# Attention and mixer kernel on one core: hand order kept through the first block's steps, conversions of weights between softmax steps, weight transfers three entries ahead

## Chip, core and metric

The kernel runs on one core of a Trainium2 chip. The metric is device microseconds of one execution; a kernel is timed several times and the median is given. A profile is taken in an execution of its own.

## What is computed

```
# q, k, v: (8 batches, 8 heads, 576, 64), chunks of 64 along the sequence
scores = scale * matmul(q_c, k_c^T)                    # 64 x 64 per chunk
attn   = softmax(scores); x = matmul(attn, v_c)        # back to (8, 576, 512)
h      = relu(x^T @ w_tok1) @ w_tok2                   # 576 -> 256 -> 576, over the sequence
u      = x + h^T
out    = u + relu(u @ w_ch1) @ w_ch2                   # 512 -> 1536 -> 512, over the channels
```

The four weight matrices come in double precision. Everything else is in single precision.

## The kernel before

**The matmuls.** A product is made of three matmuls in fp32r, a reduced form of fp32: a number is split into a kept half and a low half, and kept×kept, kept×low and low×kept are added (`THREE`). The kept half is a ScalarE cast; the low half is the number less the kept one, on VectorE (on GpSimd for `xl`).

**Channel part.** The 4608 columns of the eight batches are cut into nine blocks of 512. A block has twelve steps f. In step f, `ch1` (L534) multiplies `u` by a slice of 128 columns of w_ch1 (twelve matmuls at L540), ScalarE writes the kept half of the relu, `gh` (L545), and VectorE the low half, `gl` (L546). `ch2` (L553) multiplies these by the matching slice of w_ch2 (twelve matmuls at L568) into four accumulators. On TensorE, `ch2` of step f - 1 stands behind `ch1` of step f. At a block's end VectorE and GpSimd add `u` and the sync queue writes the output (L577, L579, L584). `SEGMENTS` gives the order: steps 0 to 7 of block 0, all of block 1, steps 8 to 11 of block 0, then blocks 2 to 8.

**Attention and token part.** A tile is two chunks, 128 rows of the sequence, with eight heads. Two batches make nine tiles: four of the one, the fifth half and half, four of the other. The first five are worked ahead of everything (L619 to L646), with transposes on TensorE. The later ones are put into steps of the channel part, given by `SLOTS`; for block 0 these are steps 0, 2, 4 and 6. `attention(k)` (L657) finishes tile j and begins the next tile, i: `pt` of j (L344, ScalarE), scores of i and the product with V of j in one PSUM tile (`attn_both`, L285, L305), loads of a later tile, the row maximum `mx` (L266), the difference (L269), the exponential (L273, ScalarE), the transposition of the probabilities of i by way of DRAM (`attn_far`: VectorE transposes in blocks, L316, a store `far`, four loads into `pf`), the sums, and then for j the division (`attn_o`), `xh`, `xl` and a transposition of x by way of DRAM into `xt` (`attn_x`). Between two blocks, at a turn, `tok1` (L482, matmuls at L459) and `tok2` (L507, L522) make the `u` of the next block: `u` (L527, VectorE), `uh` (L531, ScalarE), `ul` (L532, VectorE). The first block has forms of its own (`tok1_first`, `tok2_first`). The fifth tile is stored half by half for its two batches (`ready`, `attn_stack`, with a cast at L417).

**The weights.** They are handed over as 64-bit words in 29 entries of `plan`: five for the token weights, then c1_0, c1_1, c2_0, c1_2, c2_1 and so on. `fetch` (L108) issues an entry's transfer on the sync queue, `AHEAD` entries ahead of its use, into one of `RAW_BUFS` buffers. The words become a single on the chip: ScalarE writes `wtop` and `low` (L131, L132, `words_scalar`, called by `prepare`), VectorE clamps (L135), puts the sign in (L148), shifts (L141) and adds (L155); then come the kept cast (L203, ScalarE) and the low half (L209, VectorE). `conversion` (L171) is a generator that issues the VectorE steps one at a time: clamp of entry i, sign of i - 1, shift of i, add of i - 1 (with its cast), low half of i - 2. `convert(n)` takes n of them; ten make two entries. `ch1` and `ch2` take as many as they still need for their slice.

**What sets the order.** The sync queue and TensorE follow the program's order all through. ScalarE and VectorE follow it only through the start (`by_hand`, closed at L648); from there on a scheduler orders them, with what the start issued kept in front. `FIRST_FILL`, `PREPARE` and `END_FILL` say how many conversions stand between the softmax steps of the start. `CONVERT` asks for ten per step in block 0 and four in block 1. The splits of the token weights (`split`, L682) are issued in step 5.

Of the kernel before, what the change touches and what calls it, by code (L numbers as in the profile page):

```python
# [16 lines left out]
P = 128  # L17
B, H, S, D = 8, 8, 576, 64
CH = 64
# [26 lines left out]
CONVERT = {(0, 0): 10, (1, 0): 4, (0, F0): 0}  # L46

AHEAD = 7
RAW_BUFS = 8
KEPT_GROUPS = (13, 21)  # L50
# [3 lines left out]
FIRST_FILL = (3, 4, 5, 5, 6)  # L54
PREPARE = (0, 2, 2, 2, 2)
END_FILL = (4, 3, 2)
# [3 lines left out]
def attention_mixer_kernel(ctx, tc, qk_in, v_in, w1_in, w2_in, wc1_in, wc2_in, out):  # L60
# [57 lines left out]
    def words_scalar(i):  # L118
# [194 lines left out]
    def far_out(src, tag="far"):  # L313
# [6 lines left out]
        far = dram.tile([P, DM], F32, tag=tag, name="far")  # L320
# [101 lines left out]
    def attn_x(b, i):  # L422

        for t, rows, j in mix_tiles(b):
# [3 lines left out]
            while first < end:  # L428
# [3 lines left out]
                far_in(tiles[t]["x"], xt(k)[:, at:at + n], part)  # L432
# [101 lines left out]
    def ch1(u, f):  # L534
# [3 lines left out]
        for k in range(NDT):  # L538
            for q, (wi, ui) in enumerate(THREE):
# [3 lines left out]
                )  # L543
        gh, gl = [pool.tile([P, N], F32R, tag=tag, name=tag) for tag in ("gh", "gl")]
# [69 lines left out]
    attn_load(first[4])  # L614
    warm(12)
# [27 lines left out]
    rs, us = {0: r}, {0: block_u()}  # L643
# [5 lines left out]
    after = ExitStack()  # L649
    for engine in engines:  # L650
        ins = [i for i in nc.cur_bb.bb.instructions if i.engine == engine][-1]
        after.enter_context(tc.issue_after(ins))

    attn_load(second[1])
    order = [t for b in range(1, B) for t in batch_tiles(b)]

    def attention(k):  # L657
# [8 lines left out]
        if i is not None:  # L666
            attn_p(i)
            attn_far(i)
            attn_z(i)
        if j is not None:  # L670
            attn_o(j)
            attn_end(j)
            for b in range(1, B):
                if j in [t for t, _, _ in mix_tiles(b)] and (b % 2 == 0 or j % NTILE != 4):
                    attn_x(b, j)
# [6 lines left out]
    def split():  # L682
        for i in range(token):
# [103 lines left out]
```

## Time and profile before

| | |
|---|---|
| Median of 3 runs | 834.29 us (833.8, 834.29, 835.13) |
| Profiled execution | 832.94 us, span 831.2 us |
| Mean granted TensorE clock | 0.967 |
| Busy share of the span: TensorE, VectorE, ScalarE, GpSimd | 94%, 45%, 26%, 10% |
| Chain that ended last | TensorE 82%, DMA 7%, VectorE 5%, ScalarE 2% |
| Start of `ch1` of step 0, block 0 | 56.42 us |
| End of `ch1` of step 7, block 0 | 134.41 us |

The span runs from the first instruction to the last; the execution's time is 1.7 us more. PE is TensorE, DVE VectorE, ACT ScalarE, POOL GpSimd, SPq the sync queue. A row of the timeline has the start, the duration, the engine, the line and operation, output and inputs, and in brackets the idle time ahead of it with what ended it. In a row of stretches the four busy engines follow the length.

### The profile page before, as it was taken

The page shows a single profiled execution, that of the slowest core. Times are in us where ns is not written, and L with a number is a line of the kernel's source. Part 1 is how long each engine was busy: PE and PEld are TensorE (multiplying, and loading weights), DVE is VectorE, ACT ScalarE, POOL GpSimd, SP SyncE. Part 2 cuts the span into 40 slices and gives each one's busy share as a digit, 9 for nine tenths or more (in the row PEclk, how much of TensorE's full clock was granted, in tenths as well). Part 3 has the DMA queues.
Part 4 walks back from the last instruction along what each step waited for, and adds up shares of the span by engine and source line. Part 5 has one row for each costly group of instructions (what it writes and reads, how often), then busy time and mean ns, then how long its engine had stood idle before and what let it go on. Part 6 is the DMA issues. An engine that isn't in the chain of part 4 may idle for free.

```text
span 831.2 us, 13454 instructions
## 1 busy us (share of the span) xinstructions
PE 780.8 (94%) x5552; PEld 633.7 (76%) x5552; DVE 374.7 (45%) x660; ACT 214.1 (26%) x361; POOL 86.1 (10%) x74
## 2 busy tenths in 40 slices
PE   6685679999999999999999999999999999999997
PEld 4354567888888888888888888888888888887886
DVE  4979786423534433454443435534442323115112
ACT  4655453212231222122322221222212211012100
POOL 0000100200210000211020011200030102004000
PEclk7696799999999999999999999999999999999999
DMA  9634654232463333145403340534133201001001
GB/s 358 237 123 140 204 200 143 83 97 83 140 186 106 103 107 123 53 151 159 140 28 123 127 137 16 171 129 160 32 118 118 77 1 51 0 1 50 1 1 51
DMA packets 67373, 89.90 MB, mean 108 GB/s; under 512 B 7984, under 2 KB 40240, under 8 KB 67312
## 3 DMA queue, kind: packets, MB, share of 16 engines
q1 hardware_dynamic: 67312, 89.05, 32.1%
q8 instruction: 43, 0.70, 0.4%
q14 instruction: 18, 0.15, 0.1%
HBM read 61.10 MB, written 27.00 MB: 106 GB/s over the span
## 4 chain that ended last, share of the span: by engine, by line
PE 82%; DMA 7%; DVE 5%; ACT 2%; SPq 1%; issue 1%; ACTq 0%; DVEq 0%
PE acc L568 35%; PE ps_c L540 33%; PE ps_t L522 6%; PE ps_t L459 5%; DMA raw<-in_wc 2%; PE ps_sv L293 2%; PE ps_sv L305 2%; DMA far<-blocks 2%; DMA qk<-in_qk 2%; DMA raw<-in_w 1%; SPq L327 1%; DVE u L527 1%; DVE wtop L148 1%; ACT wtop L131 1%; ACT low L132 1%
## 5 line engine op out<-in xcount | busy, mean ns | idle before, releaser
L568 PE MATMUL acc<-gh,kept 128*128 128x512 f32 x864 | 274.8, 400 | 0.0
L540 PE MATMUL ps_c<-uh,kept 128*128 128x512 f32 x864 | 267.8, 391 | 0.0
L546 DVE SCALAR_TENSOR_TENSOR gl<-ps_c,gh 128x512 fp32r<-128x512 f32 x108 | 74.5, 690 | 335.7 <-ACT gh L545 326.1
L540 PEld LDWEIGHTS ps_c<-uh,kept 128*128 128x128 f32 x864 | 162.9, 189 | 34.8
L568 PEld LDWEIGHTS acc<-gh,kept 128*128 128x128 f32 x864 | 161.9, 190 | 34.9
L568 PE MATMUL acc<-gl,kept 128*128 128x512 f32 x432 | 170.7, 395 | 0.0
L540 PE MATMUL ps_c<-ul,kept 128*128 128x512 f32 x432 | 168.8, 391 | 0.3 <-DVE ul L505 0.3
L545 ACT ACTIVATE gh<-ps_c 128x512 fp32r<-128x512 f32 x108 | 64.5, 597 | 316.6 <-PE ps_c L540 314.3
L568 PEld LDWEIGHTS acc<-gl,kept 128*128 128x128 f32 x432 | 82.4, 191 | 18.2
L540 PEld LDWEIGHTS ps_c<-ul,kept 128*128 128x128 f32 x432 | 81.4, 188 | 17.8 <-DVE ul L505 0.8
L402 POOL TENSOR_TENSOR xl<-x,xh 128x512 fp32r<-128x512 f32 x28 | 36.6, 1308 | 447.1 <-ACT xh L401 420.1
L579 POOL TENSOR_TENSOR o<-o,ul 128x512 f32<-128x512 f32 x32 | 43.5, 1388 | 236.9 <-DVE o L577 236.9
L522 PE MATMUL ps_t<-kept,rh 128*128 128x448 f32 (+7 forms) x224 | 49.6, 314 | 6.2 <-DVE u L527 6.2
L522 PEld LDWEIGHTS ps_t<-kept,rh 128*128 128x128 f32 x224 | 37.1, 189 | 9.3 <-DVE u L527 7.9
L305 PE MATMUL ps_sv<-v,pt 64*64 64x64 f32 x992 | 21.2, 225 | 22.8 <-ACT pt L344 22.8
L344 ACT COPY pt<-pf 128x512 f32<-128x512 f32 x31 | 19.2, 620 | 79.4 <-DMA pf<-far 79.4
L273 ACT ACTIVATE pr<-pr 128x512 f32<-128x512 f32 x36 | 22.7, 632 | 63.1 <-DVE pr L269 63.0
L531 ACT CAST uh<-u 128x512 fp32r<-128x512 f32 x32 | 19.9, 621 | 68.4 <-DVE u L527 68.4
L527 DVE TENSOR_TENSOR u<-ps_t,xt 128x512 f32<-128x512 f32 x32 | 22.1, 689 | 32.3 <-PE ps_t L522 32.0
L305 PEld LDWEIGHTS ps_sv<-v,pt 64*64 64x64 f32 x992 | 18.2, 140 | 23.8 <-ACT pt L344 23.4
L459 PE MATMUL ps_t<-xh,kept 128*128 128x512 f32 x112 | 34.9, 393 | 0.0
L522 PE MATMUL ps_t<-kept,rl 128*128 128x448 f32 (+7 forms) x112 | 34.7, 311 | 0.0
(74 smaller groups left out, 614.5 us busy)
## 6 DMA issues: line engine op xcount, KB each, us to landing
qk<-in_qk SPq DMA_DIRECT2D x36, 512.0 KB, 3.9
far<-blocks SPq DMA_DIRECT2D x63, 256.0 KB, 2.1
raw<-in_wc SPq DMA_DIRECT2D x24, 512.0 KB, 6.2
v<-in_v SPq DMA_DIRECT2D x36, 260.0 KB, 4.3
out<-o SPq DMA_DIRECT2D x32, 256.0 KB, 2.0
pf<-far SPq DMA_DIRECT2D x124, 64.0 KB, 1.9
xt<-far SPq DMA_DIRECT2D x96, 64.0 KB, 2.0
xt<-far SPq DMA_DIRECT2D x64, 32.0 KB, 1.8
```

What stands on the lines that cost most here:

```text
L273: nc.scalar.activation(out=pr, in_=pr, func=AF.Exp, scale=1.0 / float(D) ** 0.5)
L305: nc.tensor.matmul(ps[c * CH:(c + 1) * CH, a, (NHP + hp) * D:(NHP + hp + 1) * D], lhsT=t["pt"][a * CH:(a + 1) * CH, hp, c * CH:(c + 1) * C ...
L402: nc.gpsimd.tensor_tensor(out=xl, in0=t["x"], in1=xh.bitcast(F32), op=ALU.subtract)
L459: nc.tensor.matmul(ps, lhsT=lhsT, rhs=rhs, start=(n == 0 and q == 0), stop=(n == len(mt) - 1 and q == len(terms) - 1),)
L522: nc.tensor.matmul(ps[:, at:at + n], lhsT=lhsT[:, cols], rhs=rhs, start=(q == 0), stop=(q == len(terms) - 1),)
L527: nc.vector.tensor_tensor(out=u.rearrange("p (i c) -> p i c", c=BK), in0=ps.rearrange("p (i c) -> p i c", c=BK), in1=xt(k)[:, :, m], op=AL ...
L531: nc.scalar.copy(out=uh[:, m], in_=u)
L540: nc.tensor.matmul(ps, lhsT=weights["c1", f][:, wi, k * P:(k + 1) * P], rhs=u[ui][:, k], start=(k == 0 and q == 0), stop=(k == NDT - 1 and ...
L545: nc.scalar.activation(out=gh, in_=ps, func=AF.Relu)
L546: nc.vector.scalar_tensor_tensor(out=gl, in0=ps, scalar=0.0, in1=gh.bitcast(F32), op0=ALU.max, op1=ALU.subtract)
L568: nc.tensor.matmul(accs[e], lhsT=weights["c2", f][:, wi, e * P:(e + 1) * P], rhs=g[gi], start=(first and q == 0), stop=(end and q == 2),)
L579: nc.gpsimd.tensor_tensor(out=o, in0=o, in1=ul, op=ALU.add)
```

## The change

Numbers: `AHEAD` goes from 7 to 3, `RAW_BUFS` from 8 to 7; there are five buffers for `wtop` and four for `low`. `FIRST_FILL` falls from 23 conversions to 10, `END_FILL` from 4, 3 and 2 (the last four times) to 3, 3 and 2.

Order: ScalarE and VectorE stay in the program's order through steps 0 to 7 of block 0; the scheduler takes over at block 1 (`seg == 1`). In each of these steps but the last, `ch1` takes six conversions between its matmuls and its `gh` and `gl`, and four more come behind the step's other work (`STEP_FILL`). The token weights are split in steps 1, 3 and 5 (`SPLITS`). `attention(0)` stands ahead of `tok2_first`, and `ready` in step 1. In `attention`, `attn_o` of the tile that is finished comes ahead of `attn_far` of the next. The load of the fifth tile's other half is a function of its own, called in the start. Loads into `xt` for a later block than the one that they are made for are kept in `late` and issued behind the last `ch2` of the turn; `xt` has one buffer.

```
-CONVERT = {(0, 0): 10, (1, 0): 4, (0, F0): 0}
+CONVERT = {(1, 0): 4}
-AHEAD = 7
-RAW_BUFS = 8
-KEPT_GROUPS = (13, 21)
+AHEAD = 3
+RAW_BUFS = 7
+KEPT_GROUPS = (13, 17, 21, 25)
-FIRST_FILL = (3, 4, 5, 5, 6)
+FIRST_FILL = (2, 2, 2, 2, 2)
-END_FILL = (4, 3, 2)
+END_FILL = (3, 3, 2)
+STEP_FILL = (6, 4)
+SPLITS = {1: (0, 1), 3: (2, 3), 5: (4,)}
...
+    def stack_load(i, halves=range(2)):
+        t = tiles[i]
+        t["xc"] = pool.tile([P, DM], F32, tag="xc", name="xc", bufs=1)
+        for c in halves:
+            rows, other = slice(c * CH, (c + 1) * CH), slice((1 - c) * CH, (2 - c) * CH)
+            nc.sync.dma_start(out=t["xc"][other], in_=t["x"][rows])
...
-                far_in(tiles[t]["x"], xt(k)[:, at:at + n], part)
+                if wait and k > b:
+                    late.append((tiles[t]["x"], k, at, n, part))
+                else:
+                    far_in(tiles[t]["x"], xt(k)[:, at:at + n], part)
...
-    def ch1(u, f):
+    def ch1(u, f, fill=0):
...
+        if fill:
+            prepare()
+            convert(fill)
         gh, gl = [pool.tile([P, N], F32R, tag=tag, name=tag) for tag in ("gh", "gl")]
...
+    second = batch_tiles(1)
+    attn_load(second[0])
     warm(12)
...
-    second = batch_tiles(1)
-    attn_load(second[0])
     convert(END_FILL[0])
     attn_o(first[last], (1, 1))
+    stack_load(first[4], range(1, 2))
+    attn_load(second[1])
     convert(END_FILL[1])
...
-    for m in range(NDT):
-        convert(END_FILL[2])
-        tok2_first(r, m, us[0], ps_acc.tile([P, N], F32, tag="acc", name="ps_t2"))
-    start_ps.close()
-    by_hand.close()
...
-            attn_p(i)
+            attn_p(i, fill)
+        if j is not None:
+            attn_o(j)
+        if i is not None:
             attn_far(i)
             attn_z(i)
         if j is not None:
-            attn_o(j)
             attn_end(j)
...
+    attention(0)
+    for m in range(NDT):
+        tok2_first(r, m, us[0], ps_acc.tile([P, N], F32, tag="acc", name="ps_t2"))
+        convert(END_FILL[2])
+    start_ps.close()
...
+        if seg == 1:
+            by_hand.close()
...
         for f in range(lo, hi):
-            g = ch1(us[k], f)
+            g = ch1(us[k], f, STEP_FILL[0] if seg == 0 and f < hi - 1 else 0)
+            if seg:
+                convert(CONVERT.get((k, lo), 0))
+            elif f == 1:
+                ready()
+            if seg == 0:
+                for i in SPLITS.get(f, ()):
+                    split(i)
...
-            convert(CONVERT.get((k, lo), 0))
-            if (k, f) == (0, F0 - 3):
-                split()
             if f - lo in slots:
                 attention(done)
                 done += 1
+            if seg == 0 and f < hi - 1:
+                prepare()
+                convert(STEP_FILL[1])
...
+            if turn:
+                for far, to, at, n, rows in late:
+                    far_in(far, xt(to)[:, at:at + n], rows)
+                late.clear()
```

What this does to the rows of an engine, at three places. The number behind `ps_c`, `ps_t` or `kept` tells tiles apart. ScalarE, before, in steps 1 and 2 of block 0; `gh` is the kept half of a step's relu:

```order
L344 COPY pt<-pf 128x4x4x32
L417 CAST xr<-xc 64x512
L203 CAST kept_796<-wtop 128x512
L132 ACTIVATE low<-raw 128x512
L203 CAST kept_796<-wtop 128x512
L131 ACTIVATE wtop<-raw 128x512
L132 ACTIVATE low<-raw 128x512
L203 CAST kept_796<-wtop 128x512
L131 ACTIVATE wtop<-raw 128x512
L132 ACTIVATE low<-raw 128x512
L545 ACTIVATE gh<-ps_c_766 128x512
L203 CAST kept_796<-wtop 128x512
```

ScalarE, in the changed kernel, in step 2 (the lines of the file have moved: L133, L134 and L205 are the words and the cast, L564 is `gh`, L346 `pt`):

```order
L133 ACTIVATE wtop<-raw 128x512
L134 ACTIVATE low<-raw 128x512
L205 CAST kept_512<-wtop 128x512
L133 ACTIVATE wtop<-raw 128x512
L134 ACTIVATE low<-raw 128x512
L205 CAST kept_512<-wtop 128x512
L564 ACTIVATE gh<-ps_c_794 128x512
L346 COPY pt<-pf 128x4x4x32
L275 ACTIVATE pr<-pr 128x512
L403 CAST xh<-x 128x512
```

Before, `pt` of this tile stood ahead of `gh` of step 2, among conversions of several entries. Now a step has the words and casts of two entries, then `gh`, and `pt`, the exponential and `xh` behind it.

VectorE, before, at the turn from block 0 to block 1; the four `u` come from `tok2`, the four `o` are the parts of block 0 that the end of `ch2` of step 7 gives:

```order
L527 TENSOR_TENSOR u<-ps_t_1404,xt 128x512
L532 TENSOR_TENSOR ul<-u,uh 128x512
L527 TENSOR_TENSOR u<-ps_t_1417,xt 128x512
L527 TENSOR_TENSOR u<-ps_t_1403,xt 128x512
L532 TENSOR_TENSOR ul<-u,uh 128x512 x2
L527 TENSOR_TENSOR u<-ps_t_1403,xt 128x512
L577 TENSOR_TENSOR o<-acc,uh 128x512 x2
L532 TENSOR_TENSOR ul<-u,uh 128x512
L577 TENSOR_TENSOR o<-acc,uh 128x512 x2
```

VectorE, in the changed kernel, from the third of these `u` on (L543 `u`, L548 `ul`, L596 `o`; L137, L150, L143, L157 and L211 are conversions):

```order
L543 TENSOR_TENSOR u<-ps_t_1352,xt 128x512
L548 TENSOR_TENSOR ul<-u,uh 128x512
L543 TENSOR_TENSOR u<-ps_t_1352,xt 128x512
L548 TENSOR_TENSOR ul<-u,uh 128x512
L211 TENSOR_TENSOR kept_1089<-wtop,kept_1089 128x512
L137 TENSOR_SCALAR wtop<-wtop 128x512
L150 SCALAR_TENSOR_TENSOR wtop<-raw,wtop 128x512
L143 TENSOR_SCALAR wtop<-wtop 128x512
L157 ISA wtop<-wtop,low 128x1024
L211 TENSOR_TENSOR kept_1269<-wtop,kept_1269 128x512
L596 TENSOR_TENSOR o<-acc,uh 128x512 x4
```

Six conversions stand between the last `ul` and the four `o`, and each `u` stands behind the `ul` of the one before. The second of the low halves is that of c2_7, which `ch2` of step 7 reads.

The sync queue, in the changed kernel, from the fifth tile's loads up to step 1 (L237 and L242 load a tile's q, k and v, L116 weights, L323 is a store `far`, L329 the loads from it):

```order
L237 DMA qk<-in_qk 128x1024
L242 DMA v<-in_v 128x520
L237 DMA qk<-in_qk 128x1024
L242 DMA v<-in_v 128x520
L116 DMA raw<-in_wc 128x1024 x8
L413 DMA xc<-x 64x512
L237 DMA qk<-in_qk 128x1024
L242 DMA v<-in_v 128x520
L323 DMA far<-blocks 128x512
L329 DMA pf<-far 32x4x128 x4
L116 DMA raw<-in_wc 128x1024
```

Before, twelve weight entries stood ahead of the second of these pairs of loads, and `xc` stood behind the first `far` and its `pf`.

More of the change, by code (lines that the diff above doesn't have):

```diff
@@ L420, in attn_stack, with attn_x @@
             )
-    def attn_x(b, i):
+    late = []
+    def attn_x(b, i, wait=False):
         for t, rows, j in mix_tiles(b):
@@ L642, in attention_mixer_kernel, with attention @@
     nc.vector.tensor_scalar_max(out=r[1], in0=sums[1], scalar1=0.0)
-    rs, us = {0: r}, {0: block_u()}
-    for m in range(NDT):
-        convert(END_FILL[2])
-        tok2_first(r, m, us[0], ps_acc.tile([P, N], F32, tag="acc", name="ps_t2"))
-    start_ps.close()
-    by_hand.close()
[L649 to L654, printed above, removed]
     order = [t for b in range(1, B) for t in batch_tiles(b)]
-    def attention(k):
+    def attention(k, fill=0):
         i = order[k] if k < len(order) else None
@@ L680, in ready, with split @@
         attn_x(0, first[4])
-    def split():
-        for i in range(token):
-            split_high(i)
-            split_low(i)
-        for c in range(2):
-            kept_half = half_kept[:, c]
-            nc.vector.tensor_scalar(
-                out=kept_half, in0=weights["t1", 4][:, 1].bitcast(F32),
-                scalar1=half_mask[:, c:c + 1], scalar2=None, op0=ALU.mult,
-            )
-            half_low.append(kept_half)
-    by_hand.enter_context(tc.manual_schedule(engines={nc.tensor.engine}))
-    done, pend, accs = 0, None, []
-    attention(done)
-    done += 1
-    ready()
+    def split(i):
+        split_high(i)
+        split_low(i)
+        if plan[i][0] == ("t1", 4, 1):
+            for c in range(2):
+                nc.vector.tensor_scalar(
+                    out=half_kept[:, c], in0=weights["t1", 4][:, 1].bitcast(F32),
+                    scalar1=half_mask[:, c:c + 1], scalar2=None, op0=ALU.mult,
+                )
+                half_low.append(half_kept[:, c])
+    rs, us = {0: r}, {0: block_u()}
+    attention(0)
[3 more added lines that the diff above has]
+    start_ps.close()
+    done, pend, accs = 1, None, []
+    after = None
     for seg, (k, lo, hi) in enumerate(SEGMENTS):
         slots = SLOTS.get((k, lo), SLOTS[3 - (k + 1) % 2] if 2 <= k < B - 1 else ())
-        for f in range(lo, hi):
-            g = ch1(us[k], f)
+        if seg == 1:
+            by_hand.close()
+            after = ExitStack()
+            for engine in engines:
+                ins = [i for i in nc.cur_bb.bb.instructions if i.engine == engine][-1]
+                after.enter_context(tc.issue_after(ins))
+            by_hand.enter_context(tc.manual_schedule(engines={nc.tensor.engine}))
+        if seg == 2:
+            after.close()
+        for f in range(lo, hi):
+            g = ch1(us[k], f, STEP_FILL[0] if seg == 0 and f < hi - 1 else 0)
[6 more added lines that the diff above has]
+                    split(i)
             if (k, f) == (0, NFC - 1):
```

17 lines of the change are left out of this document (9 added, 8 removed).

## The prediction

> **What bounds the kernel now.** I read the table of stretches first: where TensorE is idle, and what is busy there.
>
> ```profile
> span 831.2 us, 13454 instructions
> 0.00:56.42 56.42, 42.79 (x460) 25.40 (x460) 40.87 (x90) 31.00 (x54) 0.91 (x10) 0.79 0.69 264
> 56.42:134.41 77.99, 52.89 (x427) 41.81 (x426) 67.76 (x132) 39.39 (x70) 3.87 (x3) 0.80 0.51 169
> 160.00:831.00 671.00, 660.35 (x4550) 545.53 (x4548) 251.49 (x419) 136.72 (x227) 74.14 (x56) 1.00 0.28 89
> ```
>
> The columns after the length are busy TensorE, its weight loads, VectorE, ScalarE, GpSimd, the clock, the DMA share and rate. From 160 us on TensorE is busy 98% at full clock: nothing done to the other engines can shorten that part. Up to 134.41 us, the end of the first eight steps of block 0, it is idle for 13.6 + 25.1 = 38.7 us, and VectorE is busy 87% of the second stretch. So I asked TensorE's timeline what it waited for there.
>
> ```profile
> 24.40 1.14 PE L363 MATMUL ps_v<-v,pt 64*64 64x65 f32 x32 [0.84 <-ACT pt L348]
> 34.50 0.65 PE L335 MATMUL ps_t<-ident,pr 128*128 128x128 f32 x4 [1.95 <-ACT pr L273]
> 38.85 1.14 PE L363 MATMUL ps_v<-v,pt 64*64 64x65 f32 x32 [3.70 <-ACT pt L348]
> 56.42 0.74 PE L540 MATMUL ps_c<-uh,kept 128*128 128x512 f32 x2
> 71.69 1.13 PE L305 MATMUL ps_sv<-v,pt 64*64 64x64 f32 x32 [8.77 <-ACT pt L344]
> 90.97 1.13 PE L305 MATMUL ps_sv<-v,pt 64*64 64x64 f32 x32 [7.54 <-ACT pt L344]
> 108.56 0.69 PE L305 MATMUL ps_sv<-v,pt 64*64 64x64 f32 x32 [2.65 <-ACT pt L344]
> 126.47 0.69 PE L305 MATMUL ps_sv<-v,pt 64*64 64x64 f32 x32 [3.86 <-ACT pt L344]
> ```
>
> Each row is one batch of matmuls, with the idle time ahead of it and its releaser. In block 0 every long wait stands before the second product of attention (L305), which I call V5 to V8 after its tile; it waits for `pt`, ScalarE's copy of the probabilities. The chain of waits gives the rest of the turn to block 1.
>
> ```profile
> 127.16 4.53 PE acc L568 x12
> 131.69 2.72 PE ps_c L540 x12
> 134.41 6.45 PE ps_t L459 x28
> 140.87 2.72 PE acc L568 x12
> 143.59 5.01 PE ps_t L522 x30
> 151.30 2.72 PE acc L568 x12
> 154.02 5.44 PE ps_c L540 x24
> ```
>
> Twelve matmuls take 2.72 us, but 4.53 after V8's wait of 3.86: a wait costs some 1.8 us more in low clock. From 134.41 to 154.02 TensorE hardly stops. A new time for V8, and what is added behind it, is therefore the whole answer.
>
> **The change part by part.**
>
> *Start, up to ch1 of step 0.* The kept casts (L203) and low halves (L209) of the token weights leave the start, and FIRST_FILL falls from 23 conversions to 10. V2's and V4's waits (0.84 and 3.70) were for a `pt` behind such casts on ScalarE, and the 1.95 for a `pr` behind conversions on VectorE; all three go. The transposes of tile 2 come about 0.5 earlier, by one cast, and no more, because ScalarE is still held there by the second token matrix's transfer. Sum 7.0: ch1(0) starts at 49.4 instead of 56.42. The bounds are 3.7 (V4's alone) and 8.8 (with the 2.28 that I leave to the transfer, less the 0.5). Tile 5's two loads now stand ahead of the first channel weights on the sync queue; ScalarE reaches those weights after the transfers, so I cost that at nothing; without that cover it is their 0.77 MB at the first stretch's 264 GB/s, an estimate of 2.9 us.
>
> *V5.* Prices in the hand order come from rows where instructions stand close.
>
> ```profile
> 35.71 0.42 DVE L135 TENSOR_SCALAR wtop<-wtop 128x512 f32<-128x512 f32 x1
> ...
> 38.18 0.42 DVE L135 TENSOR_SCALAR wtop<-wtop 128x512 f32<-128x512 f32 x1
> 34.55 0.64 DVE L155 CUSTOM_DVE_ANT_0 wtop<-wtop,low 128x1024 uint16<-128x1024 uint16 x1
> 35.22 0.62 ACT L203 CAST kept<-wtop 128x512 fp32r<-128x512 f32 x1 [0.78 <-DVE wtop L155]
> 71.02 0.62 ACT L344 COPY pt<-pf 128x512 f32<-128x512 f32 x1 [3.31 <-DMA pf<-far]
> 253.49 0.69 DVE L527 TENSOR_TENSOR u<-ps_t,xt 128x512 f32<-128x512 f32 x1 [3.08 <-PE ps_t L522]
> 254.21 0.62 ACT L531 CAST uh<-u 128x512 fp32r<-128x512 f32 x1 [4.53 <-DVE u L527]
> 254.86 0.69 DVE L532 TENSOR_TENSOR ul<-u,uh 128x512 fp32r<-128x512 f32 x1 [0.69 <-ACT uh L531]
> 171.61 0.68 DVE L266 TENSOR_REDUCE mx<-ps_sv 128x8 f32<-128x512 f32 x1
> ...
> 175.76 0.20 DVE L283 RECIPROCAL zs<-zs 128x8 f32<-128x8 f32 x1
> ```
>
> One weight block's five VectorE instructions take 2.47 (35.71 to 38.18: three of 0.6, two of 0.33). A cast follows its add by 0.67, holds ScalarE 0.52, and gl follows gh by 0.63. V follows its `pt` by 0.67 (71.02 to 71.69). The eight attention instructions take 4.4 (171.61 to 175.96). The last `ul` of tok2_first starts 0.75 after the matmuls (0.1, then 254.21 to 254.86), at 50.15; behind it the hand order has seven instructions up to an add at 53.5, whose cast now stands ahead of gh on ScalarE: gh at 54.7, gl at 55.4, `pt` at 55.2, V5 at 55.9. Tile 5's scores and exponential now stand ahead of tok2_first, so the far transfers that made V5 late are issued some 14 us before V5 and no longer hold it. Against 71.69 that is 15.8 earlier.
>
> *Steps 0 to 6, the other way.* Each step now has ten conversion calls in hand order, two weight blocks (4.94). With gl (0.6) and attention (4.4) an even step is 9.9 of VectorE work; step 1 with the stack, a transpose and two token splits 8.0; steps 3 and 5 with token splits 7.2 and 6.2. Six steps: 51.1. The order adds waits. gh of each step stands behind the cast of the last add, so gl comes 1.85 after the add and not 1.2: 0.65 six times, 3.9. Queued behind gh are `pt`, the exponential and the `xh` cast; V waits for `pt`; and `mx` for the whole of V, though it reads only the scores:
>
> ```profile
> 92.17 0.69 DVE L266 TENSOR_REDUCE mx<-ps_sv 128x8 f32<-128x512 f32 x1 [2.25 <-PE ps_sv L305]
> ```
>
> It started at 92.17, when V6 (90.97 + 1.13) ended, long after its scores. From gl to the end of V is 0.54 + 0.69 or 1.13, so `mx` loses 0.7 once and 1.1 twice: 2.9. In step 1 the stack waits 0.5 for its ScalarE cast. Then the transfers, which AHEAD = 3 fetches one step ahead, behind both far round trips of the tile:
>
> ```profile
> 277.94 0.33 SPq L321 DMA_DIRECT2D far<-blocks  x1
> ...
> 285.81 0.38 SPq L235 DMA_DIRECT2D qk<-in_qk  x1
> 92.98 1.99 SPq L114 DMA_DIRECT2D raw<-in_wc  x4
> 97.05 0.66 ACT L131 ACTIVATE wtop<-raw 128x512 f32<-128x512 f32 x1 [2.79 <-DMA raw<-in_wc]
> ```
>
> From the first far store to the next load the queue needs 7.9, and the raw block 4.1 more: the words of steps 3 and 5 start some 5 us into those steps, and hold casts and gh by 0.9 and 1.7: 2.6. Together 51.1 + 3.9 + 2.9 + 0.5 + 2.6 = 61.0 from V5 to V8, where before has 54.8. V8 is at 116.9 instead of 126.47: 9.6 earlier. Bounds: no wait but VectorE's own work (51.1), or raw blocks that land 2.1 later in three steps (67).
>
> *Behind V8.* V8 now waits over 6 us and runs cold like V5 (1.13 for 0.69): 0.45 later. ch2(5), ch1(7), tok1, ch2(6) and tok2 as before, except that `u` of the third tile now stands behind `ul` of the second: 0.6. Then the new wait: the low half of c2_7, which ch2(7) needs from its second matmul, is converted only behind the last `ul`. From the end of tok2: `u` at 0.04, `uh` 0.72 and `ul` 1.37 later (253.49 to 254.86), then low, clamp, sign, shift, add, low: 0.6 + 0.6 + 0.33 + 0.6 + 0.33 + 0.6 + 0.68, end at 5.2. ch2(7) stood at 151.30 right behind tok2; it now stops 5.0 us after one matmul, and runs in low clock: 1.7. Queued behind it on TensorE is all of block 1. Of 9.6 there is left 9.6 - 0.45 - 0.6 - 6.7 = 1.85.
>
> *Block 1.* The weight blocks that are left, six or seven, are converted beside block 1, where TensorE's matmuls hide them, but for the first gl: between the four `o` and it stand nine conversions, 4.4. It is ready 0.7 + 4.4 + 0.6 = 5.7 after ch2(7); TensorE needs it 5.9 after (5.44 and two matmuls). GpSimd's four adds run just then:
>
> ```profile
> 152.79 5.50 POOL L579 TENSOR_TENSOR o<-o,ul 128x512 f32<-128x512 f32 x4 [16.02 <-DVE o L577]
> 135.14 1.63 POOL L402 TENSOR_TENSOR xl<-x,xh 128x512 fp32r<-128x512 f32 x1 [16.55 <-ACT xh L401]
> 135.75 1.56 DVE L155 CUSTOM_DVE_ANT_0 wtop<-wtop,low 128x1024 uint16<-128x1024 uint16 x1
> ```
>
> Beside one GpSimd add the conversion took 1.56, not 0.64: 0.9 lost. If the adds hold the conversions to their own end, gl is 1.9 late, with low clock 3.6; if none meets, nothing. I take 1.2. The Trainium skill (Advanced Engine Details and Errata, Mode Summary) says that the second Vector SBUF port is shared with GpSimd, so that GpSimd instructions and two-port Vector instructions block each other; the row agrees, and the rule speaks against the change, which puts conversions next to the adds. By it the whole 3.6 is the estimate, and the sum would be 2.4 worse.
>
> *Later blocks.* The deferred xt loads stand behind the output stores, up to 20 on the queue. Where the next far store follows soonest, it is issued here:
>
> ```profile
> 517.37 4.54 SPq L584 DMA_DIRECT2D out<-o  x4
> 526.98 0.33 SPq L321 DMA_DIRECT2D far<-blocks  x1
> ```
>
> Twelve loads of 0.45 take 5.4 from 521.9: 527.3, then two more loads, a far store 1.2 later than 526.98. Its `pt` has about as much slack, so I cost it at nothing, and at 1.7 of low clock if the slack is gone. One xt buffer is enough, since the loads follow the last reader.
>
> Sum: 1.85 - 1.2 = 0.6 faster. The profiled execution took 832.94 (span 831.2), the median of the runs is 834.29: 832.3 in a profile, **833.7** as a median.
>
> **The rivals.** *VectorE's work alone sets the steps.* For it: 87% busy in the second stretch; against it: the `mx` row and the casts' order, which are fixed by data and by hand. The waits of 9.9 between V5 and V8 go: 834.3 - 0.6 - 9.9 = 823.8. The Trainium skill (Perfetto Trace Analysis, Identifying the Most-Contended Engine) would have it so: take the engine of the highest occupancy as the bottleneck. Here VectorE's rows bear that out for its own stretch, but not for a hand order that stops it. Chance 0.22.
>
> *The first gl's of block 1 (slower).* For it: the add's row. The last two raw blocks also stand behind the four part stores, which wait for the adds, and eight xt loads, and their words stand ahead of the third gh. Price: 3.6 for the first gl and 1.5 for the third, less the 1.2 counted: 3.9, so 837.6. It decides when the first gl starts later than 5.2 us after ch2(7). Chance 0.18.
>
> *Three blocks ahead is too few (slower).* The page has the raw blocks' median to landing at 6.2:
>
> ```profile
> raw<-in_wc SPq DMA_DIRECT2D x24, 512.0 KB, 6.2
> ```
>
> With that, and not 4.1, steps 1, 3 and 5 lose 0.9, 2.1 and 2.1: 838.8. Against it: fewer are in flight at once than when these were taken. Chance 0.12.
>
> **How the numbers follow.** My forecast has 0.43; its own range is 830 to 838 (the start 3.3 the wrong way or 1.8 the right way, block 1 between 0 and 3.6). About 0.2% (1.7 us) is what a measurement of this kernel tells from no change. Of the 0.43, 0.14 lies below that, 0.18 within, 0.11 above; the first rival is all faster, the second 0.14 slower and 0.04 within, the third slower; 0.05 for other things is split: faster 0.38, same 0.24, slower 0.38. Both signs hold much of it. The range, 824 to 840, takes in the rivals' centres but leaves out the tails of the first.
>
> **What would show it.** Right: ch1(0) near 49, V5 near 56, V8 near 117, a stop of about 5 us in ch2(7) behind VectorE's `kept`, and VectorE idle ahead of `mx` and gl in every step. Wrong: V5 to V8 in under 55 us, ch2(7) without a stop, or V5 after 60.

## The result, and the profile after

The changed kernel takes 853.84 us (median of four runs, 852.96 to 855.66); beside it the kernel before takes 834.35. The ratio is 1.0236, with a 95% interval of 1.0217 to 1.0254: slower by 2.4%. The forecast was 833.7, with a range of 824 to 840. The profiled execution took 855.66, 22.7 more than that of before; 19.5 of this is the difference of the medians, and the rest is the spread of single runs.

The table of stretches, as before: busy TensorE, its weight loads, VectorE, ScalarE, GpSimd, the clock, the DMA share and rate.

```profile
span 853.7 us, 13430 instructions
...
0.00:56.42 56.42, 40.97 (x537) 25.48 (x538) 36.96 (x80) 27.79 (x47) 0.91 (x10) 0.97 0.67 248
56.42:134.41 77.99, 52.68 (x371) 41.85 (x371) 60.63 (x113) 36.76 (x65) 5.20 (x4) 0.80 0.53 173
160.00:831.00 671.00, 656.72 (x4481) 537.34 (x4480) 261.16 (x441) 141.33 (x235) 74.20 (x56) 0.99 0.28 89
```

The two early stretches together hold no fewer of TensorE's matmuls than before (908 against 887). The last, where the forecast saw nothing to lose, has 3.6 us less of busy TensorE and 69 matmuls fewer (4481 against 4550). So the place to look is behind 160 us. TensorE's timeline gives the long waits, from V5 to the last (seven short ones for `u`, 6.2 together, stand behind 160 us in both kernels and are left out):

```profile
55.52 0.69 PE L307 MATMUL ps_sv<-v,pt 64*64 64x64 f32 x32 [3.08 <-ACT pt L346]
77.33 1.14 PE L307 MATMUL ps_sv<-v,pt 64*64 64x64 f32 x32 [10.20 <-ACT pt L346]
100.19 1.14 PE L307 MATMUL ps_sv<-v,pt 64*64 64x64 f32 x32 [8.78 <-ACT pt L346]
121.09 1.14 PE L307 MATMUL ps_sv<-v,pt 64*64 64x64 f32 x32 [6.33 <-ACT pt L346]
152.14 0.80 PE L587 MATMUL acc<-gh,kept 128*128 128x512 f32 x1 [5.00 <-DVE kept L211]
164.20 0.50 PE L587 MATMUL acc<-gl,kept 128*128 128x512 f32 x1 [1.60 <-DVE gl L565]
373.63 0.69 PE L307 MATMUL ps_sv<-v,pt 64*64 64x64 f32 x32 [1.66 <-ACT pt L346]
549.28 1.14 PE L307 MATMUL ps_sv<-v,pt 64*64 64x64 f32 x32 [2.76 <-ACT pt L346]
646.97 0.78 PE L307 MATMUL ps_sv<-v,pt 64*64 64x64 f32 x32 [2.09 <-ACT pt L346]
```

V5, the stop of 5.00 in ch2(7) and the wait for the first gl stand where they were forecast. The last three rows were not forecast: waits for `pt` in blocks 3, 5 and 6, of which the kernel before has none. Every step of the channel part has the same matmuls in both kernels, so the lag of one trace behind the other can be read step by step. Each row is the start of a step's first matmul, or of V:

| Place | Before | After | Lag | Forecast lag |
|---|---|---|---|---|
| ch1(0), block 0 | 56.42 | 48.49 | -7.9 | -7.0 |
| V5 | 71.69 | 55.52 | -16.2 | -15.8 |
| V8 | 126.47 | 121.09 | -5.4 | -9.6 |
| Block 1, step 0 | 153.86 | 156.51 | +2.7 | -1.9 |
| Block 1, step 2 | 162.02 | 166.61 | +4.6 | -0.6 |
| End | 831.17 | 853.73 | +22.6 | -0.6 |

From block 1, step 2, to the end the lag grows by 18.0. It jumps in three places, by 3.5 (block 3, step 4), 5.8 (block 5, step 4) and 3.9 (block 6, step 5), 13.2 together: the three waits, 6.5, and the low clock behind them. The other 4.8 creep in, some two nanoseconds with each matmul.

**The three waits.** The sync queue at the second attention step of block 3, before:

```profile
357.00 0.33 SPq L321 DMA_DIRECT2D far<-blocks  x1
359.08 1.80 SPq L327 DMA_DIRECT2D pf<-far  x4
```

And in the changed kernel:

```profile
358.36 3.88 SPq L329 DMA_DIRECT2D xt<-far  x8
362.34 0.37 SPq L237 DMA_DIRECT2D qk<-in_qk  x1
362.81 0.38 SPq L242 DMA_DIRECT2D v<-in_v  x1
363.27 0.38 SPq L323 DMA_DIRECT2D far<-blocks  x1
369.42 1.75 SPq L329 DMA_DIRECT2D pf<-far  x4
```

The `pf` loads are issued when the far store has landed: 2.1 us after its issue before, 6.2 after. The store is not issued late: 9.8 behind the block's start before (347.22), 9.9 after (353.39). It lands late, because half a microsecond ahead of it stand 0.77 MB of q, k and v, which the deferred xt loads have pushed there. In blocks 5 and 6, with the same loads just ahead, it lands 4.6 and 4.5 after its issue, and there the issue is 2.8 and 1.1 later too. The Trainium skill (DMA: Bandwidth & Descriptors, Queues, rings and completion order) says that each DMA engine takes the descriptors of a ring in order; these rows agree, and e1 below tries it.

**The creep.** Both stretches are in block 7, with TensorE never idle and the clock at 1.00. Before:

```profile
690.00:740.00 50.00, 50.00 (x222) 41.42 (x221) 8.12 (x13) 5.98 (x10) 3.66 (x3) 1.00 0.06 22
```

After:

```profile
712.00:762.00 50.00, 50.00 (x219) 40.85 (x218) 7.64 (x12) 5.99 (x10) 3.19 (x3) 1.00 0.12 39
```

In 50 us 222 matmuls before, 219 after. The starts of the trace show which are slow; here are the distances in ns within three groups of ch2 in block 8 of the changed kernel, with the bytes by which gh and gl start off a multiple of 128 in a partition, by the tile addresses of the built program:

```
gh 64, gl  0: 237 235 228 237 235 228 237 235 228 237 235 228
gh  0, gl 64: 227 226 237 241 224 226 229 233 232 231 236 231
gh  0, gl  0: 227 226 227 227 226 227 227 226 227 227 226 227
```

Over the whole trace, ch2 groups with both on a multiple take 227.3 ns a matmul (5 groups), the others 230.9 (94), and the ch1 that follows takes some 227 or 229.8. Before it is 227.2 (79) and 231.6 (25). The change altered no address by intent. Tiles of v take 2080 bytes, those of mx and zs 32, so a tile behind them starts off a multiple; which of them came to stand ahead of gh and gl is not shown. The mean goes from 227.7 to 230.2, which over the 2592 matmuls of ch1 and ch2 makes 6 us, an estimate beside the 4.8 that the lag shows from block 1 on.

### The profile page after: what moved, and what is told of

Its sections match the earlier page's. It is cut to its first block, busy times and chain, and to the rows that moved or that the text cites. A ratio compares the mean times of both kernels' runs of the same rounds, so it can differ in the third digit from the quotient of the medians.

```text
span 853.7 us, 13430 instructions
## 1 busy us (share of the span) xinstructions
PE 788.4 (92%) x5552; PEld 635.6 (74%) x5552; DVE 378.1 (44%) x660; ACT 214.7 (25%) x361; POOL 85.6 (10%) x74
## 4 chain that ended last, share of the span: by engine, by line
PE 79%; DMA 8%; DVE 8%; ACT 3%; issue 1%; SPq 1%; ACTq 0%; DVEq 0%
PE acc L587 33%; PE ps_c L556 30%; PE ps_t L475 5%; PE ps_t L538 5%; DMA raw<-in_wc 3%; DMA far<-blocks 2%; PE ps_sv L307 2%; PE ps_sv L295 2%; DMA v<-in_v 2%; DVE u L543 1%; SPq L329 1%; DVE wtop L150 1%; PE ps_t L517 1%; DMA pf<-far 1%; DVE wtop L157 1%
## 5 line engine op out<-in xcount | busy, mean ns | idle before, releaser
L587 PE MATMUL acc<-gh,kept 128*128 128x512 f32 x864 | 282.0, 408 | 5.0 <-DVE kept L211 5.0
L587 PEld LDWEIGHTS acc<-gh,kept 128*128 128x128 f32 x864 | 165.2, 195 | 42.7 <-DVE kept L211 5.4
L587 PE MATMUL acc<-gl,kept 128*128 128x512 f32 x432 | 173.6, 402 | 1.6 <-DVE gl L565 1.6
L564 ACT ACTIVATE gh<-ps_c 128x512 fp32r<-128x512 f32 x108 | 64.5, 597 | 316.4 <-PE ps_c L556 316.4
L556 PEld LDWEIGHTS ps_c<-ul,kept 128*128 128x128 f32 x432 | 81.5, 189 | 18.8
L275 ACT ACTIVATE pr<-pr 128x512 f32<-128x512 f32 x36 | 22.7, 631 | 68.7 <-DVE pr L271 66.5
L346 ACT COPY pt<-pf 128x512 f32<-128x512 f32 x31 | 19.2, 619 | 74.0 <-DMA pf<-far 71.7
L543 DVE TENSOR_TENSOR u<-ps_t,xt 128x512 f32<-128x512 f32 x32 | 22.0, 689 | 31.9 <-PE ps_t L538 31.7
```

The source lines that it names most:

```text
L275: nc.scalar.activation(out=pr, in_=pr, func=AF.Exp, scale=1.0 / float(D) ** 0.5)
L543: nc.vector.tensor_tensor(out=u.rearrange("p (i c) -> p i c", c=BK), in0=ps.rearrange("p (i c) -> p i c", c=BK), in1=xt(k)[:, :, m], op=AL ...
L556: nc.tensor.matmul(ps, lhsT=weights["c1", f][:, wi, k * P:(k + 1) * P], rhs=u[ui][:, k], start=(k == 0 and q == 0), stop=(k == NDT - 1 and ...
L564: nc.scalar.activation(out=gh, in_=ps, func=AF.Relu)
L587: nc.tensor.matmul(accs[e], lhsT=weights["c2", f][:, wi, e * P:(e + 1) * P], rhs=g[gi], start=(first and q == 0), stop=(end and q == 2),)
```

## The experiments

Each was timed beside the kernel before. The ratios have their 95% intervals.

| Run | Median | Ratio to before |
|---|---|---|
| changed kernel | 853.84 | 1.0236 (1.0217 to 1.0254) |
| e1, far store first | 852.28 | 1.0211 (1.0192 to 1.0230) |
| e2, xt loads in mid-block | 844.11 | 1.0115 (1.0094 to 1.0136) |
| e3, step 6 converts more | 844.02 | 1.0105 (1.0069 to 1.0141) |
| e4, before with the deferral | 844.11 | 1.0099 (1.0068 to 1.0129) |
| e5, aligned | 843.85 | 1.0111 (1.0088 to 1.0134) |
| e6, before aligned | 833.37 | 0.9995 (0.9976 to 1.0014) |
| e7, AHEAD = 4 | 846.54 | 1.0141 (1.0115 to 1.0168) |
| e8, pt first | 845.63 | 1.0141 (1.0117 to 1.0165) |
| e9, conversions behind | 854.27 | 1.0242 (1.0225 to 1.0258) |
| e10, scheduler from step 0 | 840.88 | 1.0074 (1.0051 to 1.0097) |
| e11, four mends joined | 824.93 | 0.9902 (0.9879 to 0.9925) |
| e12, joined, conversions behind | 828.06 | 0.9925 (0.9907 to 0.9942) |
| e13, two mends | 835.02 | 1.0015 (1.0006 to 1.0024) |
| e14, joined, pt first, AHEAD = 4 | 817.96 | 0.9804 (0.9788 to 0.9820) |

**The late V of blocks 3, 5 and 6 (e1, e2, e4).**

```
 e1, in attention():
-        if j is not None and k + 1 < len(order):
+        loads = j is not None and k + 1 < len(order)
+        if loads and k < 5:
             attn_load(order[k + 1])
...
             attn_far(i)
             attn_z(i)
+        if loads and k > 4:
+            attn_load(order[k + 1])
```

> The changed kernel, with one thing moved: from the sixth attention step on (from block 1), the loads of q, k and v of the next tile are issued behind the probabilities' far store and its four pf loads, not ahead of them. Theory A (in blocks 3, 5 and 6 the far store is issued 0.5 us behind 0.77 MB of loads and lands 4.5 to 6.2 us after its issue instead of 2.0, so pt and V are late): the store is issued 0.9 sooner and lands in 2.0 again, the three stalls go, which cost 3.5, 5.8 and 3.9: 13.2 less, 840.6. Theory B (the queue is simply late, because the deferred xt loads stand ahead): only the 0.9 of two issues is won in each of the three places, 851.

In time it is nearest to theory B, but the trace shows both. The far store of block 3 in e1, with the xt loads but not q, k and v ahead of it:

```profile
364.88 0.34 SPq L323 DMA_DIRECT2D far<-blocks  x1
367.62 1.73 SPq L329 DMA_DIRECT2D pf<-far  x4
369.45 0.38 SPq L237 DMA_DIRECT2D qk<-in_qk  x1
369.92 0.38 SPq L242 DMA_DIRECT2D v<-in_v  x1
```

It lands in 2.7, and the lag jumps by 0.8, 2.0 and 0.5 in the three places instead of 3.5, 5.8 and 3.9: the loads ahead of the store made 9.9 of the 13.2. What ate the gain is a row of the table of waits of e1 behind 160 us (total, times, longest):

```profile
PE ps_sv L295 <- DMA qk<-in_qk: 6.9, 8, 1.9
```

The next tile's q and k now come behind the round trip, and TensorE waits for them eight times.

```
 e2:
-            if turn:
-                for far, to, at, n, rows in late:
+            if seg and f == (7 if k == 1 else 6):
+                for far, to, at, n, rows in [x for x in late if x[1] == k + 1]:
                     far_in(far, xt(to)[:, at:at + n], rows)
-                late.clear()
+                late[:] = [x for x in late if x[1] != k + 1]
```

> The changed kernel, with the deferred xt loads not issued at the turn but in the middle of the next block (behind ch2 of step 5, in block 1 of step 6). Theories A and B (the deferred loads bring q, k, v and the far store together on the queue): all three stalls go, 840.6. Theory C (the stalls come from something else in the change, such as the single xt buffer or attn_o ahead of attn_far): no change, 853.8.

9.7 won by the medians. None of the three jumps is left; the waits for `pt` behind 160 us fall from 6.5 to one of 1.2, at a new place in block 5. So the deferral to the turn is the cause, and theory C falls. e4 puts the same deferral on the kernel before, by the change's own lines for `late` and `far_x`:

> The kernel before, with the deferral of xt loads alone (loads for a later block collected and issued behind the last ch2 of the turn; twelve far buffers for x; xt keeps two buffers). Theories A and B: stalls ahead of V in blocks 3, 5 and 6 as in the changed kernel, 13 more: 847.5, at least 842 if the kernel before has more slack there. Theory C: no change, 834.3.

10 lost, between the two. The jumps are 4.7 in block 5 and 4.1 in block 6; in block 3 the store lands 4.4 after its issue, and no wait follows there. The deferral costs this without the rest of the change.

**The stop in ch2(7) (e3).**

```
-                convert(STEP_FILL[1])
+                convert(STEP_FILL[1] + 6 * (f == hi - 2))
```

> The changed kernel, with six more conversions at the end of step 6 of block 0 (ten instead of four), so that the low half of c2_7 is made ahead of the turn. Theory D (the stop of 5.00 us in ch2(7), with 1.7 of low clock behind it, comes from these six standing behind the last ul): 6.7 less, and up to 1.9 more because the first gl of block 1 stands behind fewer conversions: 845 to 847. Rival: the six hold gl of step 7 and the first rl on VectorE instead, and tok2 waits as long: 852 or more.

The turn costs 0.7 instead of 7.8, as theory D has it. The first gl did not get better but worse (the lag jumps by 3.0 there instead of 1.9): the conversions now start earlier in the run of GpSimd's adds, and three of them meet it instead of two. In the changed kernel, the second conversion behind the four `o`, and the adds:

```profile
158.29 1.77 DVE L150 SCALAR_TENSOR_TENSOR wtop<-raw,wtop 128x512 int32<-128x512 int32 x1
...
154.24 5.27 POOL L598 TENSOR_TENSOR o<-o,ul 128x512 f32<-128x512 f32 x4 [27.80 <-DVE o L596]
```

In e3, where three conversions meet the adds, and what TensorE waits for gl:

```profile
151.08 1.26 DVE L137 TENSOR_SCALAR wtop<-wtop 128x512 f32<-128x512 f32 x1
152.27 1.77 DVE L150 SCALAR_TENSOR_TENSOR wtop<-raw,wtop 128x512 int32<-128x512 int32 x1
153.96 1.77 DVE L211 TENSOR_TENSOR kept<-wtop,kept 128x512 fp32r<-128x512 f32 x1
...
157.99 0.50 PE L587 MATMUL acc<-gl,kept 128*128 128x512 f32 x1 [2.72 <-DVE gl L565]
```

Beside an add, L137 takes 1.26 instead of 0.42, L150 and L211 1.77 instead of 0.68. The Trainium skill (Advanced Engine Details and Errata, Mode Summary) says that GpSimd and two-port Vector instructions block each other on a shared port; the row of L137 agrees. L150 and L211, which read two tensors, are stretched too, and of such instructions that sentence says nothing. Smaller jumps in blocks 3, 5 and 6 (7.2 instead of 13.2) have a part in e3's 9.8 too.

**The pace (e5, e6).**

```
+    def small(tag):
+        t = pool.tile([P, 32], F32, tag=tag, name=tag)
+        return t[:, :2 * NHP].rearrange("p (a b c) -> p a b c", a=2, b=NHP)
...
-        v = pool.tile([P, 2, NHP, DV], F32, tag="v" if i > 4 else "v0", name="v", bufs=2 if i > 4 else 5)
+        v = pool.tile([P, 544], F32, tag="v" if i > 4 else "v0", name="v", bufs=2 if i > 4 else 5)
+        v = v[:, :VW].rearrange("p (a b c) -> p a b c", a=2, b=NHP)
...
-        mx = pool.tile([P, 2, NHP, 1], F32, tag="mx", name="mx")
+        mx = small("mx")
```

zs and zi are changed as mx is.

> The changed kernel, with small tiles made larger so that every tile starts at a multiple of 128 bytes in a partition (mx, zs and zi 128 bytes instead of 32, v 2176 instead of 2080); the work is the same. Theory E (1084 of the 1296 ch2 matmuls of the changed kernel read a gh or gl that starts 32 or 64 bytes off such a multiple, 176 before; such a group runs at up to 236 ns a matmul instead of 227 and slows the next ch1 too, 230.2 on average against 227.7 before): the mean goes to 226.7, so 3.5 ns less in 2592 matmuls, 9 us: 845. Rival F (the slower pace comes from something else, such as the weights in five tiles instead of three): no change, 853.8.

10.0 won. The same stretch of block 7:

```profile
702.00:752.00 50.00, 50.00 (x223) 41.40 (x222) 7.37 (x11) 5.99 (x10) 2.90 (x3) 1.00 0.11 37
```

223 matmuls instead of 219, and 227.2 ns on average instead of 230.2: 7.7 us over 2592. In this trace block 3 has no wait either; blocks 5 and 6 still jump, by 5.1 and 4.0. So the pace makes 7.7 of the 10.0 by this estimate, and the rest may be these smaller waits. Rival F falls, since the weights still lie in five tiles.

> The kernel before, with the same larger small tiles, so that every gh and gl starts at a multiple of 128 bytes. Theory E: 227.7 ns goes to 226.7 in 2592 matmuls, 2.6 less: 831.7. Rival F: 834.3.

Not shown in the time: the ratio's interval includes 1. In the trace the pace goes from 227.7 to 227.2, which would be worth 1.3, an estimate.

**The steps of block 0 (e7 to e10).** VectorE's work and time between V5 and V8, before:

```profile
71.69:126.47 54.78, 40.73 (x325) 32.44 (x325) 45.85 (x88) 27.22 (x49) 3.87 (x3) 0.84 0.58 197
```

After:

```profile
55.52:121.09 65.57, 40.26 (x324) 31.78 (x324) 52.75 (x100) 32.65 (x58) 3.89 (x3) 0.80 0.57 186
```

The third pair is VectorE: 6.9 us more work, brought over from the start, and 3.9 more idle. The idle time has three kinds. All of them stand in step 4:

```profile
95.43 0.66 ACT L133 ACTIVATE wtop<-raw 128x512 f32<-128x512 f32 x1 [5.67 <-DMA raw<-in_wc]
97.18 0.69 DVE L211 TENSOR_TENSOR kept<-wtop,kept 128x512 fp32r<-128x512 f32 x1 [1.49 <-ACT kept L205]
99.67 0.69 DVE L565 SCALAR_TENSOR_TENSOR gl<-ps_c,gh 128x512 fp32r<-128x512 f32 x1 [1.80 <-ACT gh L564]
101.40 0.69 DVE L268 TENSOR_REDUCE mx<-ps_sv 128x8 f32<-128x512 f32 x1 [1.04 <-PE ps_sv L307]
```

ScalarE waits for a raw block and holds the cast and gh; gl waits for gh behind the cast; mx waits for V. Between V5 and V8 gl waits 0.58 behind the cast in each of six steps (3.5), and mx waits 2.7 for V. What is left of the waits of `kept` and gl is due to raw blocks and makes 5.3: 0.8 up to the gl of step 2, 2.7 up to that of step 4, 1.8 up to that of step 6 (the prediction counts them to steps 1, 3 and 5). The sync queue shows why the blocks for step 4 are late:

```profile
69.64 0.38 SPq L323 DMA_DIRECT2D far<-blocks  x1
75.12 1.74 SPq L329 DMA_DIRECT2D xt<-far  x4
...
81.39 0.33 SPq L323 DMA_DIRECT2D far<-blocks  x1
85.32 2.03 SPq L329 DMA_DIRECT2D pf<-far  x4
...
91.36 1.80 SPq L116 DMA_DIRECT2D raw<-in_wc  x4
```

The first of these far stores lands 5.5 after its issue, behind 1.0 MB of weights. So the next loads, 1.8 MB, are issued late and have not all landed when the second store is issued; it lands in 3.9. The weights for step 4 stand behind that: they are issued 10.0 after it, at 91.36, and then land in 4.0 (the words start at 95.43). In e3, whose order is the same up to step 6, the two stores land sooner, in 3.8 and 2.7:

```profile
70.84 0.33 SPq L323 DMA_DIRECT2D far<-blocks  x1
74.69 1.74 SPq L329 DMA_DIRECT2D xt<-far  x4
...
82.11 0.33 SPq L323 DMA_DIRECT2D far<-blocks  x1
84.83 2.03 SPq L329 DMA_DIRECT2D pf<-far  x4
```

There the waits for raw blocks make 2.6, none of it up to the gl of step 2, and V5 to V8 takes 62.9.

```
 e7: -AHEAD = 3     +AHEAD = 4
 e8, in attention(), and ahead of ch1 in the loop:
-        if j is not None:
+        if j is not None and "pt" not in tiles[j]:
             attn_t(j)
...
+            if seg == 0 and f - lo in slots:
+                attn_t(order[done - 1])
```

> The changed kernel with AHEAD = 4 instead of 3, all else the same. Theory G (words of steps 2, 4 and 6 wait for raw blocks that are issued behind both far round trips of the tile, and hold the casts, gh and pt; 5.3 of the 65.6 us from V5 to V8): one of a step's two blocks now stands ahead of the far trips and half of the 5.3 goes, 851, V8 2 to 4 earlier than 121.1. Rival (VectorE's work and the order behind it set the steps anyway): V8 at 121, 853.8.

V8 at 117.2, 3.9 earlier: theory G. The raw waits of VectorE fall from 5.3 to 1.4, though the two far stores land as late as in the changed kernel (5.6 and 4.2). From V5 to V8, with the same work:

```profile
55.60:117.20 61.60, 39.77 (x327) 31.48 (x327) 52.72 (x100) 32.96 (x58) 3.88 (x3) 0.81 0.58 186
```

The end gains 7.3 by the medians: these 3.9 and smaller later waits (6.8 instead of 13.2), less 2.3 more for the first gls of block 1.

> The changed kernel, with pt of a step's tile (ScalarE's copy) ahead of ch1's conversions, casts and gh of that step in hand order, for steps 0, 2, 4 and 6. Theory H (V waits for a pt that stands behind casts and gh though its transfer landed long before, and mx waits 1.0 for the whole of V): the waits ahead of V shrink to under 2 us, VectorE's mx starts right behind gl, V8 3 to 4 us earlier than 121.1, ch2 behind V no longer in low clock: 849. Rival (VectorE's gl is what TensorE waits for next, so nothing is won beyond mx's 3): 851; if ScalarE is held by a pt that hasn't landed, no gain, 854.

V8 is at 118.1, 3.0 earlier, but not for the reason given: V5 alone is 2.6 earlier (52.9). Between them it takes as long as without:

```profile
52.90:118.10 65.20, 40.73 (x324) 32.17 (x324) 54.15 (x103) 32.79 (x59) 3.86 (x3) 0.84 0.54 176
```

The waits of mx are gone, and the low halves wait 4.6 for casts behind raw blocks in their stead. (This window holds three instructions of VectorE more.) The median, 845.63, is 3 below what was expected, but V8 gives only 3.0 of the 8.2 won: the later waits are smaller in this trace too, 5.7 instead of 13.2.

```
 e9:  -STEP_FILL = (6, 4)     +STEP_FILL = (0, 10)
 e10: -        if seg == 1:   +        if seg == 0:      (by_hand.close(); the end of "after" one segment earlier too)
```

> The changed kernel with STEP_FILL = (0, 10) instead of (6, 4): the ten conversions of a step stand behind its gh, gl, pt and attention, none ahead; the same instructions. Theory J (the six conversions ahead of gh are what holds gh, pt and V: of the 65.6 us from V5 to V8, 12.2 are waits of VectorE, and its own work 53.4): TensorE is ahead, V waits little, V5 to V8 takes 54 to 57, V8 at 108 to 111, the end 10 earlier: 843. Rival K (VectorE and the raw blocks pace the steps all the same, and TensorE now waits for the low halves of the weights instead): V8 at 118 or later, 851 or more.

Rival K: V8 at 122.9. gh, gl and `pt` come at once, and TensorE waits for the weights, in the table of waits of e9:

```profile
PE ps_c L556 <- DVE kept L211: 18.3, 6, 5.2
```

> The changed kernel, with ScalarE and VectorE given to the scheduler from step 0 of block 0 on, as in the kernel before, and not from block 1 on; loads, deferral, AHEAD = 3 and the start stay. Theory J: the order by hand costs some 10 us between V5 and V8 (65.6 against 54.8 before); V8 at 110 to 113. Rival K (the transfers three entries ahead do it, whoever orders): V8 at 119 or later. Here 220 of the ch2 matmuls read an operand that starts off a multiple of 128 bytes, not 1084, so about 8 less come on top: 835 by J, 844 by K.

Rival K again. V8 is at 120.2, and from V5 it takes 64.5 with VectorE busy for 54.07:

```profile
55.70:120.20 64.50, 41.63 (x325) 32.73 (x325) 54.07 (x104) 31.91 (x56) 5.04 (x3) 0.81 0.44 145
```

The scheduler does little better than the order by hand. My theory J, that the hand order costs 10 us, falls. VectorE has 8.2 more to do in this stretch than before, and the stretch is 9.7 longer: the work that was moved into the steps is most of it. The 13 that e10 gains lie elsewhere: 5.4 in the pace (228.1 ns), 5.6 in the later waits (5.7 and 1.9 left of 13.2), and 1.9 at the first gl, which no longer makes TensorE wait.

**Joined (e11 to e14).** e11 is the changed kernel with e2, e3 and e5, and `by_hand.close()` not at the start of block 1 but at its step 2.

> The changed kernel with four mends joined: the deferred xt loads in the middle of the next block, six more conversions in step 6, tiles at multiples of 128 bytes, and ScalarE and VectorE in hand order for the first two steps of block 1 too, so that the first gl stands right behind the four o. By the traces there is left against the kernel before: start and V5 -16.6, steps 11.5, turn 0.7, first gl 0 (the conversions no longer stand beside GpSimd's adds ahead of it), later blocks 0 to 1.5, pace -1.3: some 5 faster than before, 829.5. If the gains overlap (a later step has slack that hides one): 834 or more.

1.0% faster than the kernel before, 4.6 us below what was expected. Here too the two far stores land sooner than in the changed kernel (4.1 and 2.9), and V5 to V8 takes 63.1. V8 is at 118.3, step 2 of block 1 6.7 ahead of before, no first gl waits, and from there to the end the lag stays within 1.4.

> The joined kernel with STEP_FILL = (0, 10) and AHEAD = 4 besides. Theory J: V8 another 10 earlier: 819 to 822. Rival K: as the joined kernel without them, less the 4 that one entry more ahead gave: 825 to 830.

3 slower than e11, within rival K's range; V8 at 119.2.

> The changed kernel with only the two costs undone that the prediction left out: the deferred xt loads in the middle of the next block, and tiles at multiples of 128 bytes. If these two are additive and independent (9.7 and 10.0 won alone): 834. If they overlap (the stalls in blocks 3, 5 and 6 were smaller in the aligned kernel, 9.1 instead of 13.2): 836 to 838. What then stays against the forecast of 833.7 is the later V8 (4.2) and the larger first gl (0.7).

835.02: the two costs that the prediction left out make 18.8 of the 19.5, and they add up to a microsecond. Of the waits for `pt` behind 160 us one of 0.7 is left.

> The joined kernel (the order of the changed one within steps, conversions ahead of gh) with AHEAD = 4 and pt ahead of the conversions. Alone they brought V8 3.9 and 3.0 earlier. If they are separate waits: V8 at 111.5, 818. If both only free the same wait of gh behind the raw blocks: V8 at 114, 821. If V8 no longer decides the turn: 824.9, as without them.

817.96, 2.0% faster than the kernel before, and V8 at 111.9. From V5 to V8:

```profile
52.70:111.90 59.20, 40.17 (x328) 31.50 (x328) 52.46 (x100) 32.97 (x58) 3.89 (x3) 0.87 0.54 176
```

Idle VectorE is down from 12.8 to 6.7. `pt` ahead of the conversions, which did nothing between V5 and V8 by itself, seems to pay once the raw blocks are there: the waits of mx (2.7 in e7) and of the low halves (4.6 in e8) are both gone. The joined kernel with AHEAD = 4 alone was not run, so the shares of the two aren't separated.

## Why the prediction was wrong, point by point

The start needs one row more, the stretch up to ch1(0) in the changed kernel; the same stretch of the kernel before is the first in the prediction's table.

```profile
0.00:48.49 48.49, 36.12 (x460) 21.86 (x461) 31.19 (x69) 23.80 (x40) 0.91 (x10) 0.96 0.75 277
```

- *Start and V5*: right in the number (48.5 for 49.4, 55.5 for 55.9), but the start's number came in part by luck. The sum took away idle time alone, 7.0. The three waits named are gone or under a microsecond, but others came (2.36 ahead of the transposes of tile 3), and TensorE is idle for 12.4 instead of 13.6. The other 6.7 us are busy time: 42.8 before, 36.1 now, for the same 460 instructions, at a granted clock of 0.96 instead of 0.79. The sum has no term for the clock of the start.
- *Steps 0 to 6*: the right mechanism, 65.6 instead of 61.0. VectorE's work was 52.75 for 51.1. Waits of gl behind the cast (3.5 for 3.9) and of mx (2.7 for 2.9) were met. The term that was mis-sized is the raw transfers: 5.3 instead of 2.6. The third rival has nearly this price, 5.1, but by luck: it rests on raw blocks that land in 6.2, and the first block of each step landed 4.5, 4.0 and 3.8 after its issue, near the 4.1 of the sum. Only for step 2 was it the landing: the second block took 7.0, which made 0.8 of the wait. The other 1.8 too much stand ahead of step 4, whose weights were issued late behind a far store that landed in 3.9 and not in 2. That is the mistake of the later blocks in small. Where the stores land sooner, in e3 and e11, the term is 2.6, as forecast.
- *Behind V8*: right. From V8 to block 1 the lag grew by 8.0, and 7.75 were forecast; the stop is 5.00 for 5.0. e3 showed its cause.
- *First gl of block 1*: 1.9 for 1.2, within 0 and 3.6. The rival's condition came, the first gl started 7.0 after ch2(7) (163.47 against 156.51, past its 5.2), but at half its price, and the third gh was not late. By the Trainium skill's rule on the shared port (Advanced Engine Details and Errata, Mode Summary) I had the whole 3.6; in the trace two conversions met an add (1.05 for 0.42, 1.77 for 0.68), which is 1.7.
- *VectorE's work alone* fell: VectorE is idle for 12.8 of 65.6 us between V5 and V8. The Trainium skill's rule (Perfetto Trace Analysis, Identifying the Most-Contended Engine) would have made 823.8 of it; here the busiest engine of the stretch was stopped by transfers, and the time lay mostly in another stretch.
- *Later blocks*: this step failed. "Its `pt` has about as much slack, so I cost it at nothing, and at 1.7 of low clock if the slack is gone." The working counted when the far store is issued, and priced each load ahead of it at its issue, 0.45. It is the landing that moved: 4.5 to 6.2 instead of 2.1, behind loads just issued; in block 5 the issue came later too, by 2.8 and not 1.2 (the twelve loads took 6.7, not 5.4). In place of nothing, or 1.7, this cost 13.2 in the trace and 9.7 to 10 by the medians of e2 and e4.
- *A term that was missing*: no line of the sum asked whether untouched matmuls keep their pace. "From 160 us on TensorE is busy 98% at full clock: nothing done to the other engines can shorten that part" was not contradicted, but the part could be lengthened, and the memory plan did so. e5 gave 10.0 back by alignment, 7.7 of it by the pace.

Without these two the time comes back near the forecast: e13 takes 835.02, 1.3 above it. That it is so near is partly luck: V8 is still 2.8 later in e13 than forecast, and against this the alignment also takes away the small creep of the kernel before (227.2 ns for 227.7, an estimate of 1.3), which the forecast didn't count. The forecast's own range was added up too narrow as well: the bounds it names for the start and block 1 reach 839.4 and not 838, and the bound of 67 for the steps, which took 65.6, is not in it.

What remains open: which of the moved tiles put gh and gl off their multiple, why the far stores land sooner in some kernels than in others whose queues have the same order, and with it why the three later waits vary from 5.7 to 13.2. Two `xt` buffers without the deferral, and AHEAD = 5, don't fit beside the rest of the change, and weren't tried.

## What to carry to other kernels

When transfers are moved on a queue, follow each to its landing: a small store that others wait for can land late behind large loads issued just ahead of it, even if its own issue has not moved. When buffers change, compare the pace of the matmuls that nobody touched, by their number in a stretch where TensorE is never idle. Work that is moved out of a stretch comes back in the next one if the same engine sets the pace there: of the conversions taken out of the start, 6.9 us came back between V5 and V8.

## What the runs showed of the hardware

A matmul of 128x512 in fp32r starts every 226.7 ns at full clock where its operands start on a multiple of 128 bytes in the partition. With the moving operand of some of a group's matmuls 32 or 64 bytes off, single distances go up to 241, the group takes 230.9 on average (94 groups), and the twelve well-placed matmuls behind it still take 229.8. A store of 256 KB landed in 2.1 us alone, in 2.7 behind eight loads of 32 and 64 KB, and in 4.5 to 6.2 with 0.77 MB of loads issued half a microsecond ahead of it. A VectorE conversion of 0.68 took 1.77 beside a GpSimd add.
